# Half blocks of attention value products as 128x64 array tiles, with masks shared out between VectorE and GpSimd and a new instruction order

## The chip, the cores and the metric

The kernel runs on one core of one Trainium2 chip. The metric is the device time in microseconds (us) of one execution. The kernel before took 412.78 us, the median of three runs (412.25 to 413.30).

Names of engines, as in the profile: PE is TensorE (matmuls), PEld its weight loads, ACT is ScalarE, DVE is VectorE, POOL is GpSimd, SP is the queue from which most DMAs are issued. PSUM is the matmuls' output memory, here eight banks of 128 partitions x 512 float32.

## The reference

Four transformer layers on one sequence of 2048 rows of 512, in the order A, B, A, B, each with a residual and a layer norm ahead. Both use 32 heads of 16.

```python
def A(x, wqkv, wo):          # linear attention
    q, k, v = heads(x @ wqkv)
    phi = lambda t: where(t > 0, t + 1, exp(t)) + 1e-6
    kv = einsum("bhsd,bhse->bhde", phi(k), v)
    z = einsum("bhsd->bhd", phi(k))
    num = einsum("bhqd,bhde->bhqe", phi(q), kv)
    den = einsum("bhqd,bhd->bhq", phi(q), z)[..., None] + 1e-6
    return merge(num / den) @ wo

def B(x, wqkv, wo):          # causal sliding window of 256
    q, k, v = heads(x @ wqkv)
    scores = einsum("bhqd,bhkd->bhqk", q, k) * 16 ** -0.5
    keep = (i - j >= 0) & (i - j < 256)
    p = softmax(where(keep, scores, -1e9))
    return merge(einsum("bhqk,bhkd->bhqd", p, v)) @ wo

for layer, w, wo in ((A, A_wqkv, A_wo), (B, B_wqkv, B_wo)) * 2:
    x = x + layer(layernorm(x), w, wo)      # layernorm eps 1e-5
```

## The kernel before

**Tiling.** The rows are 16 blocks of 128 (`t`, `j`), all in SBUF as `xres`. Projections with the rows' features as weights are made by `tok` (L412, four matmuls of 512 columns a block) or, where the result is wanted transposed, by `feat` (L426, sixteen of 128 columns). A transposed normalised block comes from a DMA transpose on SP (L383), or for a few blocks from PE (L389).

**Norm** (`norm`). Statistics (L373) and their aggregate (L374) on DVE, the addition of the epsilon on POOL or DVE (L375), the power -0.5 on POOL (L376), subtraction and scaling on DVE (L377), then the transpose. In the attention layers the transposed block goes to `xT`, a ring of `ring_x` = 3.

**Attention layer B** (`middle`). For each block j: `front` makes the residual of the layer before, the norm, and the queries and keys of a later block; `b_v` the values; `b_scores` the scores. Scores are held with keys on partitions: a key block `b` of 64 keys stands twice (two heads a group) on the 128 partitions, and its exponentials `P` (ACT, L660) cover the 320 queries that can see it, of which the last 64 (the far edge) come from `b_far` (L690, L693, exponentials L703). Scores use array tiles of 32 rows, four beside each other; in the second B layer (`merged`) the first 32 and the last 64 query columns of a key block share a pass, in tiles of 32x64.

The causal edge of a key block is masked by `mk` (DVE, L668 and L713), the far edge by `mf` (POOL L721 or DVE L722).

`b_values` (L742) makes the outputs of query block j: for each of 16 pairs of heads, a sum over six key blocks in PSUM, with `P` as weights (128 keys-and-heads x 128 queries) and the values as 34 moving columns, two of which are the softmax sums. Of the six, the key block 2j+1 is seen only by the upper 64 queries and the key block 2j-4 only by the lower 64. Each key block's stretch in `P` has therefore 64 columns of zeros behind its 320 (row step 704, second block at 384), and both are read as full blocks of 128 with the zeros in the half that they don't reach. `consts` clears the zeros once (`c24`), and a step `zero` those of the fourth buffer of the second B layer (L816). Then DVE takes reciprocals (L753) and divides (L754), half of the heads at a time, and `b_out` transposes, multiplies by `wo` and adds the residual (L585).

**Order.** Nothing is decided at run time. Each step is a node of a graph (`Graph.add`) with the engines that may do it, its reads and writes, and a key. `place` reads a packed constant `TABLE`, which has for all steps the global order, the engine of each, and the PSUM bank of each tile; `synchronise` then puts in the waits on semaphores. Each engine's list is the order of the table. `place` adds one more dependence: a step on POOL that isn't in `SHORT` waits for the last step on DVE that is in `WIDE` and stands ahead of it in the order.

```python
        if o.eng == "POOL" and o.name not in SHORT and wide and wide not in o.deps:
            o.deps.append(wide)
        if o.eng == "DVE" and o.name in WIDE:
            wide = o
```

The first load order is `x0`, the key weight (512 KB), `x1`, `x2` and `x3`, the query weight, and so on. PE begins with matmuls on zeros (L998, L274) until data are there.

Of the kernel before, what the change touches and what calls it, by code (L numbers as in the profile page):

```python
# [8 lines left out]
ACT = mybir.ActivationFunctionType  # L9
ALU = mybir.AluOpType  # L10

P = 128
# [11 lines left out]
    same=0.0, gp=1, pe_first1=5, lat_t=4300, cap_s=8, cap_d=2, cap_e=6, mode=100, sem=35, ring_x=3, wait_s=200,  # L24
# [63 lines left out]
SHORT = ("eps", "pow", "c2", "c2b", "c11", "c12", "c13", "c14")  # L88
# [141 lines left out]
class Plan:  # L230


    def __init__(self, par):
        self.par = par
        self.g = Graph()
        self.n_phi = [0, 0]
        self.early = []
        self.closing = []
        self.build()
# [43 lines left out]
    def setup(self):  # L283
# [10 lines left out]
        seq += [xs(0, 1), w("wAk", "wA", "A_wqkv", 512, 1024), xs(1, 2), xs(2, 4), w("wAq", "wA", "A_wqkv", 0, 512), xs(4, 6), xs(6, 8), xs(8, 12)]  # L294
# [4 lines left out]
        for i, (n, f, b, r) in enumerate(seq):  # L299

            begun.append(self.load(n, f, b, r, key + i if i < 8 else 100.5 + 0.5 * i, begun[i - 4:i - 3] if i >= 7 else []))
# [10 lines left out]
        pool("c2b", zero(lambda: K.ones, 1.0), key + 2, 150, wr=[("ones",)])  # L312

    def consts(self, after):
# [23 lines left out]

        pool("c14", zero(lambda: K.tri, 1.0), 161, 200, wr=[("tri",)])
# [16 lines left out]
        for q in range(2):  # L356
            for k in range(4):
# [4 lines left out]
                self.g.add("wp", {"POOL": (810, 870), "ACT": act(512)}, move, 170 + q, rd=[("wBn",)], wr=[("wBp", q, k)], after=after)  # L362
        for s in range(3):
            clear("c24", lambda s=s: K.pb[:, s, :, :, 320:384], 1024, 180, 1000,
                  rd=[("wBp", q, k) for q in range(2) for k in range(4)] if s == 2 else [],
                  wr=[("pad", s)] + [("P", s, f) for f in range(4)])


    def norm(self, t, key, xn_slot, out, wr, by_pe):
# [3 lines left out]
        self.on("DVE", "stats", lambda e: e.bn_stats(K.stats[:, t, :], K.xres[:, t, :]), key, dve(512), rd=[("xres", t)], wr=[("stats", t)])  # L373
        self.on("DVE", "aggr", lambda e: e.bn_aggr(K.mv[:, t, :], K.stats[:, t, :]), key + 0.01, (66, 150), rd=[("stats", t)], wr=[("mv", t)])  # L374
        self.g.add("eps", {"POOL": (300, 330), "DVE": (66, 150)}, lambda e, eng: e.tensor_scalar(K.ve[:, t, :], K.mv[:, t, 1:2], LN_EPS, None, op0=ALU.add), key + 0.02, rd=[("mv", t)], wr=[("ve", t)])  # L375
        self.pow = self.on("POOL", "pow", lambda e: e.tensor_tensor(K.rs[:, t, :], K.ve[:, t, :], K.negh[:], ALU.pow), key + 0.03, (640, 690), rd=[("ve", t), ("negh",)], wr=[("rs", t)])  # L376
# [27 lines left out]
    def tok(self, name, t, lhs, rhs, rd, key):  # L404
# [3 lines left out]
        for h in range(2):  # L408
# [5 lines left out]
            self.pe(name, put, key - 0.001 * h, 2, 512, rd=rd, ps=[ps])  # L414
# [29 lines left out]
    def a_k(self, t, key):  # L444
        K = self
        xT = lambda c: K.XQ[:, c, t * P:(t + 1) * P]
        ps = self.tok("k", t, xT, lambda c: K.wA[:, c, 512:1024], [("XQ", t), ("wAk",)], key)
        self.phi(ps, lambda: K.pk[:, t, :], [("pk", t)], key + 0.1, 0)
# [12 lines left out]
    def a_kv(self, t, kv, z, key):  # L461
# [12 lines left out]
        self.pe("kv", put, key, 4, 128, occ=330, rd=[("pk", t), ("vA", t), ("ones",)], ps=[kv, z], after=self.closing)  # L474
# [112 lines left out]
    def b_qkv(self, t, s, key, key2):  # L587
# [4 lines left out]
        wk = [("wBp", 1, k) for k in range(4)]  # L592
        ps = self.feat("bq", t, lambda c, f: K.wBp[:, 0, c, f * P:(f + 1) * P], xT, rd + wq, key)
        self.copy("bqe", ps, lambda: K.XQ[:, :, t * P:(t + 1) * P], lambda ps=ps: K.ps(ps).rearrange("p (f n) -> p f n", f=4), key + 0.05, 512, wr=[("XQ", t)])
        key = key2
# [37 lines left out]

    def b_scores(self, j, b, fs, key):
# [21 lines left out]
        out = lambda h, w: bass_view(K.P(sl)[:, fs[0], h, 384 * b + skip:384 * b + skip + w], [[1408, 2 * n], [1, w]])  # L656
        for h in range(2):
# [4 lines left out]
            self.on("ACT", "ex", ex, key + 0.01 * h, act(2 * ns * n), wr=[("P", sl, f, b, h) for f in fs], rd=[("P", sl, f) for f in fs], ps=[ps[2 * h], ps[2 * h + 1]])  # L662
# [3 lines left out]
        def mk(e):  # L666
            x = bass_view(K.P(sl)[:, fs[0], 0, 384 * b:384 * b + 64], [[704, 4 * n], [1, 64]])
            return e.tensor_tensor(x, x, K.tri[:, 0, :].unsqueeze(1).to_broadcast([P, 4 * n, 64]), ALU.mult)  # L668

        self.on("DVE", "mk", mk, key + 0.02, dve(256 * n, "2x"), rd=[("P", sl, f, b, h) for f in fs for h in range(2)] + [("tri",)], wr=[("P", sl, f, b, 2) for f in fs])  # L670

    def b_far(self, j, key):
# [26 lines left out]
        for h in range(2):  # L699
            def ex(e, h=h):  # L700
                i = span(two(h), lambda x: [[128, 4], x, [64, 2], [1, 64]])
                o = bass_view(K.P(sl)[:, 0, h, 256:320], [[1408, 8], [384, 2], [1, 64]])
                return e.activation(o.rearrange("p (f g) b c -> p f g b c", g=2), i, ACT.Exp, bias=0.0, scale=0.25)  # L703

            self.on("ACT", "ex", ex, key + 0.01 * h, act(1024), wr=[("F", sl, h)], rd=[("P", sl, 0)], ps=[ps[2 * h], ps[2 * h + 1]])

        for fs in ((0, 1), (2, 3)) if merged else ():
            for b in range(2):
                def mk(e, b=b, fs=fs):
                    x = bass_view(K.P(sl)[:, fs[0], 0, 384 * b + 288:384 * b + 320], [[704, 8], [-256, 2], [1, 32]])  # L710
                    o = bass_view(K.P(sl)[:, fs[0], 0, 384 * b:384 * b + 64], [[704, 8], [32, 2], [1, 32]])
# [3 lines left out]
                self.on("DVE", "mk", mk, key + 0.02 + 0.01 * b + 0.2 * fs[0], dve(512, "2x"), rd=[("P", sl, f, b, h) for f in fs for h in range(2)] + [("F", sl, 0), ("F", sl, 1), ("tri",)],  # L715
                        wr=[("P", sl, f, b, 2) for f in fs] + [("near", sl, b, fs[0])])
        for b in range(2):
            def mk(e, eng, b=b):
                x = bass_view(K.P(sl)[:, 0, 0, 384 * b + 256:384 * b + 320], [[704, 16], [1, 64]])
# [7 lines left out]
    def b_values(self, j, h, key):  # L727
        K = self
        rp = self.rp
        ps = Tile(1, K.cls)  # L730
# [354 lines left out]
```

## Time and profile before

| what | value |
|---|---|
| median of three runs | 412.78 us (412.25 to 413.30) |
| span of the profiled execution, first to last instruction | 408.7 us |
| time of the profiled execution itself | not given apart from its span |
| clock granted to PE | 1.00 throughout |
| PE busy | 396.5 us in 7997 matmuls |
| ACT busy | 355.7 us |
| DVE busy | 343.9 us |
| POOL busy | 115.7 us |
| DMA | 37.88 MB moved, most of it in packets under 2 KB |

How to read it: "busy" is the time in which an engine had an instruction under way, and a matmul's duration holds some 0.17 us of latency that overlaps with the next ones. So the pace of matmuls is read from starts, not from durations. The chain of waits goes back from the last instruction to what released it; its shares say which engine's work set the end. Rows of groups give line, engine, operation, output and inputs, shape and count, then busy us and the mean ns of one, and behind the second bar the idle time before them.

### The profile page before, as it was taken

The page shows a single profiled execution, that of the slowest core. Times are in us where ns is not written, and L with a number is a line of the kernel's source. Part 1 is how long each engine was busy: PE and PEld are TensorE (multiplying, and loading weights), DVE is VectorE, ACT ScalarE, POOL GpSimd, SP SyncE. Part 2 cuts the span into 40 slices and gives each one's busy share as a digit, 9 for nine tenths or more (in the row PEclk, how much of TensorE's full clock was granted, in tenths as well). Part 3 has the DMA queues.
Part 4 walks back from the last instruction along what each step waited for, and adds up shares of the span by engine and source line. Part 5 has one row for each costly group of instructions (what it writes and reads, how often), then busy time and mean ns, then how long its engine had stood idle before and what let it go on. Part 6 is the DMA issues. An engine that isn't in the chain of part 4 may idle for free.

```text
span 408.7 us, 18140 instructions
## 1 busy us (share of the span) xinstructions
PE 396.5 (97%) x7997; PEld 262.5 (64%) x7997; DVE 343.9 (84%) x819; ACT 355.7 (87%) x466; POOL 115.7 (28%) x185
## 2 busy tenths in 40 slices
PE   8999999999999999999999999999999999999996
PEld 3654776766575576565566777676756766566664
DVE  7985899899999898997778879988898867876675
ACT  2998769999999999999998265999999899999992
POOL 5746422113342231521322102111213123432132
PEclk9999999999999999999999999999999999999999
DMA  7794025833342443344143100345224542352463
GB/s 246 189 197 80 2 62 146 126 92 83 67 108 43 126 101 82 93 101 101 42 68 60 25 2 28 80 107 109 55 76 103 133 69 60 104 120 79 102 135 105
DMA packets 67750, 37.88 MB, mean 93 GB/s; under 512 B 48248, under 2 KB 62840, under 8 KB 67672
## 3 DMA queue, kind: packets, MB, share of 16 engines
q1 hardware_dynamic: 67328, 35.80, 38.1%
q8 instruction: 63, 1.03, 1.1%
q0 software_dynamic: 336, 0.92, 0.6%
q14 instruction: 15, 0.12, 0.1%
q10 hardware_dynamic: 8, 0.00, 0.0%
HBM read 6.29 MB, written 2.10 MB: 21 GB/s over the span
## 4 chain that ended last, share of the span: by engine, by line
PE 66%; ACT 22%; DVE 7%; DMA 2%; issue 1%; POOL 0%; SPq 0%
PE ps L412 23%; PE ps L426 16%; ACT pb L660 14%; PE ps L742 11%; PE ps L650 6%; PE ps L492 3%; ACT pb L703 3%; ACT vp L660 2%; DMA xT<-xn 2%; PE ps L693 2%; ACT tE L435 1%; PE ps L690 1%; ACT vp L703 1%; PE ps L468 1%; DVE XQ L574 1%
## 5 line engine op out<-in xcount | busy, mean ns | idle before, releaser
L660 ACT ACTIVATE pb<-ps 128x1024 bf16<-128x1024 f32 (+3 forms) x224 | 197.8, 977 | 8.3 <-PE ps L650 7.3
L742 PEld LDWEIGHTS ps<-vB,pb 128*128 128x128 bf16 x2560 | 77.9, 96 | 11.3 <-issue 3.6
L742 PE MATMUL ps<-vB,pb 128*128 128x34 bf16 x2560 | 83.7, 177 | 0.8 <-issue 0.5
L426 PE MATMUL ps<-xT,wBp 128*128 128x128 bf16 x1024 | 70.2, 219 | 0.6 <-DMA xT<-xn 0.6
L426 PEld LDWEIGHTS ps<-xT,wBp 128*128 128x128 bf16 x1024 | 58.6, 98 | 12.3 <-issue 4.2
L721 POOL TENSOR_SCALAR_AFFINE_SELECT pb<-pb 128x1024 bf16<-128x1024 bf16 x35 | 40.7, 1162 | 67.9 <-DVE pb L713 28.8
L375 POOL TENSOR_SCALAR ve<-mv 128x1 f32<-128x1 f32 x38 | 9.7, 254 | 158.3 <-DVE mv L374 157.7
L435 ACT ACTIVATE tE<-ps 128x512 bf16<-128x512 f32 x64 | 38.1, 608 | 16.6 <-PE ps L412 9.1
L703 ACT ACTIVATE pb<-ps 128x1024 bf16<-128x1024 f32 x50 | 49.2, 1053 | 2.3 <-PE ps L693 1.3
L650 PE MATMUL ps<-XQ,kB 32*128 32x256 bf16 (+2 forms) x1024 | 48.0, 262 | 2.6 <-DVE vp L603 0.6
L412 PE MATMUL ps<-wA,XQ 128*128 128x512 bf16 x192 | 49.4, 379 | 0.2 <-DVE XQ L574 0.2
L585 DVE TENSOR_TENSOR xres<-ps,xres 128x512 bf16<-128x512 f32 x63 | 42.9, 683 | 7.9 <-PE ps L412 7.6
L376 POOL TENSOR_TENSOR rs<-ve,negh 128x1 f32<-128x1 f32 x64 | 38.6, 604 | 36.1 <-DVE ve L375 31.7
L373 DVE BATCH_NORM_STATS2 stats<-xres 128x6 f32<-128x512 bf16 x64 | 43.6, 683 | 2.4 <-DMA xres<-in_A_x_dram 1.7
L426 PE MATMUL ps<-XQ,wA 128*128 128x128 bf16 x512 | 35.1, 219 | 0.1
L412 PE MATMUL ps<-wBv,xT 128*128 128x512 bf16 x128 | 35.0, 381 | 0.0
L650 PEld LDWEIGHTS ps<-XQ,kB 32*128 32x128 bf16 x1024 | 15.3, 92 | 30.7 <-ACT pb L660 9.5
L426 PEld LDWEIGHTS ps<-XQ,wA 128*128 128x128 bf16 x512 | 30.4, 98 | 5.7 <-issue 0.6
L412 PE MATMUL ps<-M,XQ 128*128 128x512 bf16 x128 | 33.7, 380 | 0.1
L412 PE MATMUL ps<-wBo,oT 128*128 128x512 bf16 x124 | 33.2, 381 | 0.3 <-ACT pb L660 0.3
L668 DVE TENSOR_TENSOR pb<-pb,tri 128x512 bf16<-128x512 bf16 x68 | 28.1, 417 | 3.8 <-ACT pb L660 3.4
L412 PEld LDWEIGHTS ps<-wA,XQ 128*128 128x128 bf16 x192 | 16.6, 97 | 18.1 <-issue 1.0
(120 smaller groups left out, 566.8 us busy)
## 6 DMA issues: line engine op xcount, KB each, us to landing
vB<-vS SPq DMA_DIRECT2D x64, 136.0 KB, 2.6
kB<-vp SPq DMA_DIRECT2D x64, 128.0 KB, 2.2
wA<-in_A_wqkv_dram SPq DMA_DIRECT2D x3, 512.0 KB, 5.2
xres<-in_A_x_dram SPq DMA_DIRECT2D x2, 512.0 KB
pb<-in_B_wqkv_dram SPq DMA_DIRECT2D x1, 1024.0 KB, 5.5
out_dram<-xres SPq DMA_DIRECT2D x8, 128.0 KB, 3.2
out_dram<-xres POOLq DMA_DIRECT2D x7, 128.0 KB, 2.8
xres<-in_A_x_dram SPq DMA_DIRECT2D x3, 256.0 KB, 3.2
```

The lines of the kernel that those rows point to most:

```text
L373: self.on("DVE", "stats", lambda e: e.bn_stats(K.stats[:, t, :], K.xres[:, t, :]), key, dve(512), rd=[("xres", t)], wr=[("stats", t)])
L376: self.pow = self.on("POOL", "pow", lambda e: e.tensor_tensor(K.rs[:, t, :], K.ve[:, t, :], K.negh[:], ALU.pow), key + 0.03, (640, 690), r ...
L412: m = e.matmul(K.ps(ps), lhs(c), rhs(c), start=c == 0, stop=c == 3)
L426: m = e.matmul(K.ps(ps)[:, f * P:(f + 1) * P], w(c, f), xT(c), start=c == 0, stop=c == 3)
L435: self.on("ACT", "E", lambda e: e.activation(K.tE[:, s, :], K.ps(ps), ACT.Exp, bias=0.0), key, act(512), wr=[("tE", s)], ps=[ps])
L585: self.on("DVE", "res", lambda e: e.tensor_tensor(K.xres[:, t, :], K.ps(po), K.xres[:, t, :], ALU.add), key, dve(512), rd=[("xres", t)], w ...
L650: m = e.matmul(K.ps(two(gq // 2)[gq % 2])[:, ns * i:ns * i + ns], K.kB[rows, j % 4, 2 * f + b, :, :], K.XQ[rows, f, q:q + ns], start=True, ...
L660: return e.activation(out(h, ns).rearrange("p (f g) c -> p f g c", f=n), i, ACT.Exp, bias=0.0, scale=0.25)
L668: return e.tensor_tensor(x, x, K.tri[:, 0, :].unsqueeze(1).to_broadcast([P, 4 * n, 64]), ALU.mult)
L703: return e.activation(o.rearrange("p (f g) b c -> p f g b c", g=2), i, ACT.Exp, bias=0.0, scale=0.25)
L721: return e.affine_select(out=x, in_=x, compare_op=ALU.is_ge, fill=0.0, base=-2, pattern=[[0, 16], [-2, 64]], channel_multiplier=1)
L742: m = e.matmul(K.ps(ps)[:, 34 * u:34 * u + 34], K.P((b // 2) % rp)[:, f, gq % 2 * 2 + gq // 2, o:o + P], K.vB[:, (b // 2) % 4, b % 2, r, : ...
```

## The change

- **Half products.** `P` has no zeros any more (row step 640, second block at 320). `b_values` makes the four whole key blocks as before (`pv`), and then the two half ones as matmuls with 64 weight columns at `tile_position=(0, 0)` or `(0, 64)`, which write only 64 partitions of the output. They form a step of their own, `pw`, one for all 16 pairs of heads (two for the very last block). Both PSUM banks of a block are closed by it, and reciprocals and divisions of both come behind it. `c24` and the `zero` of the fourth buffer are gone. Where a buffer was lent out before, the first exponentials wait for the borrowers (`taken`).
- **Masks.** `mk` may be done by POOL too (`affine_select`; in the merged layer two of them).
- **Rings.** `xT` has five buffers in place of three; the layer's `front` runs five blocks ahead, with the keys split off (`b_k`, three ahead). `xn` has six buffers, `o` and `oT` three.
- **Epsilon.** The statistics get three more columns (0, 0, 512 x 1e-5), so that the aggregate gives variance + epsilon; the step L375 is gone. The statistics are a ring of eight.
- **Start.** The key weight is loaded in halves, behind `x0`, `x1` and `x2`; the key matmuls wait for each half by itself.
- **Order.** A new `TABLE` (2538 steps in place of 2568): order, engines, banks.

```diff
-    same=0.0, gp=1, pe_first1=5, lat_t=4300, cap_s=8, cap_d=2, cap_e=6, mode=100, sem=35, ring_x=3, wait_s=200,
+    same=0.0, gp=1, pe_first1=5, lat_t=4300, cap_s=8, cap_d=2, cap_e=6, mode=100, sem=35, ring_x=5, wait_s=200,
...
-SHORT = ("eps", "pow", "c2", "c2b", "c11", "c12", "c13", "c14")
+SHORT = ("pow", "c2", "c2b", "c2z", "c2e", "c11", "c12", "c13", "c14", "c16")
...
-        seq += [xs(0, 1), w("wAk", "wA", "A_wqkv", 512, 1024), xs(1, 2), xs(2, 4), w("wAq", "wA", "A_wqkv", 0, 512), xs(4, 6), xs(6, 8), xs(8, 12)]
+        def half(h):
...
+        seq += [xs(0, 1), xs(1, 2), xs(2, 3), half(0), half(1), xs(3, 4), w("wAq", "wA", "A_wqkv", 0, 512), xs(4, 6), xs(6, 8), xs(8, 12)]
...
+        pool("c2z", lambda e: e.memset(K.stats[:, :, 6:8], 0.0), key + 3, 100, wr=[("fold", 0)])
+        pool("c2e", lambda e: e.memset(K.stats[:, :, 8:9], D * LN_EPS), key + 4, 100, rd=[("fold", 0)], wr=[("fold",)])
...
-        for s in range(3):
-            clear("c24", lambda s=s: K.pb[:, s, :, :, 320:384], 1024, 180, 1000,
...
-        self.on("DVE", "aggr", lambda e: e.bn_aggr(K.mv[:, t, :], K.stats[:, t, :]), key + 0.01, (66, 150), rd=[("stats", t)], wr=[("mv", t)])
-        self.g.add("eps", {"POOL": (300, 330), "DVE": (66, 150)}, lambda e, eng: e.tensor_scalar(K.ve[:, t, :], K.mv[:, t, 1:2], LN_EPS, None, op0=ALU.add), key + 0.02, rd=[("mv", t)], wr=[("ve", t)])
...
+        self.on("DVE", "aggr", lambda e: e.bn_aggr(K.mv[:, t, :], K.stats[:, t % 8, :]), key + 0.01, (66, 150), rd=[("stats", t % 8), ("fold",)], wr=[("mv", t)])
...
+    def taken(self, j):
+
+        return self.borrowed if j == 2 and self.rp == 3 else self.summed if j == 3 and self.rp == 4 else []
...
-        def mk(e):
...
+        def mk(e, eng):
+            x = bass_view(K.P(sl)[:, fs[0], 0, 320 * b:320 * b + 64], [[640, 4 * n], [1, 64]])
+            if eng == "POOL":
+                return e.affine_select(out=x, in_=x, compare_op=ALU.is_ge, fill=0.0, base=1, pattern=[[0, 4 * n], [2, 64]], channel_multiplier=-1)
             return e.tensor_tensor(x, x, K.tri[:, 0, :].unsqueeze(1).to_broadcast([P, 4 * n, 64]), ALU.mult)
...
-        blocks = [(2 * j, 0), (2 * j + 1, -64), (2 * j - 1, 64), (2 * j - 2, 128), (2 * j - 3, 192), (2 * j - 4, 256)]
...
-                        o = 384 * (b % 2) + c
-                        m = e.matmul(K.ps(ps)[:, 34 * u:34 * u + 34], K.P((b // 2) % rp)[:, f, gq % 2 * 2 + gq // 2, o:o + P], K.vB[:, (b // 2) % 4, b % 2, r, :], start=i == 0, stop=i == len(blocks) - 1)
...
+        ps = [Tile(1, K.cls) for _ in range(2)]
+        whole = [(2 * j, 0), (2 * j - 1, 64), (2 * j - 2, 128), (2 * j - 3, 192)]
...
+        part = [(2 * j + 1, 0, 64)] + ([(2 * j - 4, 256, 0)] if j >= 2 else [])
...
+                        m = e.matmul(K.ps(ps[f // 2])[:, cols(f, gq)], stat(b, f, gq)[:, c:c + P], vals(b, f, gq), start=f % 2 == 0 and gq == 0 and i == 0, stop=False, skip_group_check=True)
...
+        for fs in ((0, 1), (2, 3)) if apart else (range(4),):
+            def put(e, fs=fs):
+                m = None
+                for f in fs:
+                    for gq in range(4):
+                        for b, c, r in part:
+                            m = e.matmul(K.ps(ps[f // 2])[r:r + 64, cols(f, gq)], stat(b, f, gq)[:, c:c + 64], vals(b, f, gq), start=False, stop=True, skip_group_check=True, tile_position=(0, r))
+                return m
...
-            self.b_qkv(t, t % ring, k - par["k_q"], k - par["k_kv"])
+            self.norm(t, k - par["k_ao"] + 0.3, t % 4, lambda: K.xT[:, t % ring, :, :], [("xT", t % ring)], t < par["pe_first"])
+            self.b_q(t, t % ring, k - par["k_q"])
...
         for j in range(T):
+            if j + ring < T:
+                front(j + ring)
             if j + 3 < T:
-                front(j + 3)
+                self.b_k(j + 3, (j + 3) % ring, base + j + 3 - par["k_kv"])
...
-            sb("xres", [T, D]); sb("XQ", [4, S]); sb("xn", [4, D]); sb("xT", [3, 4, P]); sb("pqd", [4, P])
+            sb("xres", [T, D]); sb("XQ", [4, S]); sb("xn", [6, D]); sb("xT", [5, 4, P]); sb("pqd", [4, P])
```

More of the change, by code (lines that the diff above doesn't have):

```diff
@@ L848, in middle @@
                 self.b_far(j, base + j + 0.8)
-            for h in range(2):
-                self.b_values(j, h, base + j + (h + 1) / 2 + par["k_pv"])
-            if not last:
-                self.closing = [self.g.ops[-1]]
+            self.b_values(j, base + j + 0.5 + par["k_pv"], last and j == T - 1)
             k = base + j + 1 + par["k_wo"]
```

244 lines of the change are left out of this document (126 added, 118 removed).

## The prediction

> **What bounds the kernel now.** I read the page first: busy shares, then the chain of waits.
>
> ```profile
> PE 396.5 (97%) x7997; PEld 262.5 (64%) x7997; DVE 343.9 (84%) x819; ACT 355.7 (87%) x466; POOL 115.7 (28%) x185
> ...
> PE 66%; ACT 22%; DVE 7%; DMA 2%; issue 1%; POOL 0%; SPq 0%
> PE ps L412 23%; PE ps L426 16%; ACT pb L660 14%; PE ps L742 11%; PE ps L650 6%; PE ps L492 3%; ACT pb L703 3%; ACT vp L660 2%; DMA xT<-xn 2%; PE ps L693 2%; ACT tE L435 1%; PE ps L690 1%; ACT vp L703 1%; PE ps L468 1%; DVE XQ L574 1%
> ```
>
> TensorE (PE) is nearly always busy and makes up two thirds of the chain that ends last; ScalarE (ACT), whose exponentials are L660 and L703, makes up a fifth. Next I cut the span where the exponentials of layer 2 begin and end (60.6 and 224.6 us) and those of layer 4 (257 and 401). The columns are window, length, then busy time of PE, PEld, DVE, ACT, POOL.
>
> ```profile
> 0.00:60.60 60.60, 59.17 (x593) 35.59 (x593) 49.76 (x140) 43.76 (x76) 31.07 (x64) 1.00 0.52 129
> 60.60:224.60 164.00, 161.76 (x3276) 104.34 (x3274) 146.37 (x349) 157.34 (x188) 44.74 (x65) 1.00 0.41 90
> 224.60:257.00 32.40, 32.40 (x506) 23.97 (x504) 27.78 (x62) 17.15 (x30) 3.47 (x8) 1.00 0.07 18
> 257.00:401.00 144.00, 138.96 (x3543) 95.82 (x3541) 116.13 (x262) 136.65 (x170) 35.36 (x46) 1.00 0.41 96
> ```
>
> Layers 2 and 4 take 308 of 408.7 us, and in both PE (99% and 97%) and ACT (96% and 95%) are full together. The first layer and the stretch between are PE alone. So work taken from PE counts in full only until ACT ends last; this decides how much of the change arrives.
>
> **The value products.** Of each block j >= 2, six key blocks of 16 matmuls make the output; two of the six have only 64 useful query columns and are now padded with zeros to 128. That is 14 x 32 + 2 x 16 = 480 half products a layer, 960 in all, of the 2560 + 320 matmuls on L742. Their number stays; they become tiles of 128x64 in the left and right half of the array. What does one cost before, and what does a tile cost?
>
> ```profile
> L742 PE MATMUL ps<-vB,pb x2560: 177/177/191, 74.5 to 402.9; 128*128 128x34 bf16 x197
> L742 PE MATMUL ps<-vB,vp x320: 177/177/191, 301.6 to 402.8; 128*128 128x34 bf16 x160
> ```
>
> ```profile
> 19.77 1.34 PE ps L426 x24
> ...
> 401.27 1.79 PE ps L742 x72
> ```
>
> ```profile
> 53.82 0.24 PE L554 MATMUL ps<-ones,eps 128*32 128x128 bf16 x4
> 53.89 0.40 PE L554 MATMUL ps<-XQ,zs 128*32 128x128 bf16 x16
> 54.22 0.61 PE L412 MATMUL ps<-M,XQ 128*128 128x512 bf16 x2
> ...
> 290.60 0.71 PE L693 MATMUL ps<-XQ,kB 32*64 32x64 bf16 x64
> 291.24 1.37 PE L742 MATMUL ps<-vB,pb 128*128 128x34 bf16 x48
> 292.54 0.37 PE L650 MATMUL ps<-XQ,kB 32*128 32x224 bf16 x8
> ```
>
> The 177 ns (least, median and most of one in ns stand behind the count) are latency; the pace is 1.79 us / 72 = 24.9 ns. The group of 48 takes 1.30 us to the start of the next, which has another tiling: 1.30 - 48 x 24.9 ns = 0.105 us is the price of a change of tiling.
>
> No 128x64 tile is in this trace, so it is bounded. The denominators (L554, 128x32 tiles) start at 53.82 and end with the next start at 54.22: 0.40 us less a change of 0.1 is 0.30 for 20, 15 ns each, where one matmul of 128 columns alone takes 1.34 / 24 = 56 ns. So column tiles with all 128 rows do run beside each other. If a left and a right tile together cost one full product, a half costs 24.9 / 2 = 12.5 ns. The merged scores (L693, 32x64 tiles, which also load 64 columns) take 0.64 - 0.1 = 0.54 us for 64: 8.4 ns each, the lower end. But each row group had 16 tiles to load in these 0.54 us, 34 ns a tile if left and right load in turn: the upper end. I take 14 ns, near the denominators, because only they use all rows. Saved: 960 x (24.9 - 14) = 10.5 us (15.8 at the lower end; at the upper 8.7 are lost).
>
> The new tiles form 33 groups of their own. Unpacking both order tables of the diff and reading them against the lists of steps, I count 334 changes of tiling on PE before and 377 after (21 of the new groups run straight into a score group): 43 x 0.105 = 4.5 us back. PE sheds 10.5 - 4.5 = 6.0 us. In the chain PE has 66% and ACT 22%, so I let three quarters of it arrive: **-4.5 us** (from -8.5 to +9.9). The half products also close both banks of a block, so that the first bank's division waits for all four groups, about 32 x 24.9 ns + 0.5 us later; behind it stand only the block's output transpose, for which there are three buffers in place of two, and PE's next user of that bank. I put 0 for it, since PE has other blocks' work between; without that it is 1.3 us in each of 32 blocks, of which the chain's 11% on L742 would carry some 4.5.
>
> The page "TensorEngine Tiling (Array Packing)" of the Trainium skill, section "Restrictions and Gotchas", says that column tiling excludes the fast weight load, and "TensorE: Matmul & The Clock Gate", section "LDWEIGHTS (loading the stationary operand)", puts a plain load at columns / 1.2 ns. An estimate from these pages, 53 ns a half product if the halves load in turn, makes the half products 960 x (53 - 24.9) = 27 us dearer, and the forecast about 431 us. The L693 rows (34 ns at the most) do not show so slow a load.
>
> **ACT, DVE, GpSimd.** The engine part of the new table gives, over the whole kernel: near masks (mk) 128 on DVE before, 56 on DVE and 72 on GpSimd after; far masks (mf) 16 on DVE and 40 on GpSimd before, 26 and 30 after; the epsilon step, 26 on DVE and 38 on GpSimd, is gone.
>
> ```profile
> L668 DVE TENSOR_TENSOR pb<-pb,tri x68: 360/416/756, 65.7 to 397.0; 128x512 bf16<-128x512 bf16 x68
> L713 DVE TENSOR_TENSOR pb<-pb,tri x44: 360/417/1944, 263.1 to 390.6; 128x512 bf16<-128x512 bf16 x44
> L722 DVE TENSOR_TENSOR pb<-pb,tri x15: 660/685/1026, 88.2 to 388.0; 128x1024 bf16<-128x1024 bf16 x15
> ```
>
> ```profile
> L375 POOL TENSOR_SCALAR ve<-mv x38: 209/223/568, 3.9 to 355.0; 128x1 f32<-128x1 f32 x38
> L375 DVE TENSOR_SCALAR ve<-mv x26: 131/146/155, 5.4 to 362.3; 128x1 f32<-128x1 f32 x26
> ```
>
> ```profile
> L721 POOL TENSOR_SCALAR_AFFINE_SELECT pb<-pb x35: 1137/1147/1341, 88.9 to 397.5; 128x1024 bf16<-128x1024 bf16 x35
> ```
>
> ```profile
> L401 ACT ACTIVATE XQ<-ps 128x512 bf16<-128x512 f32 x11 | 6.6, 604 | 1.1 <-PE ps L426 1.0
> ...
> L833 ACT ACTIVATE vp<-pb 128x1152 bf16<-128x1152 bf16 x3 | 3.5, 1159 | 0.0
> ```
>
> The first six rows have least, median and most of one in ns. DVE: -72 x 0.42 + 10 x 0.69 - 26 x 0.146 = -27, and about +2 for copies that come over from ACT and +2 for the longer aggregate of nine numbers: -23 us of 344, 7%. The chain has 7% on DVE, 28.6 us; 7% of that is **-2.0** (0 to -4).
>
> GpSimd: a near mask has half the elements of a far one (1147 ns), so 0.6 to 0.9 us, say 0.75: +72 x 0.75 - 10 x 1.15 - 38 x 0.22 = +34 us, to about 150 us, 37%. It is no bound, but it works in order: behind a mask stand the reciprocal roots (L376) of the norms and the other masks, and who waits are the value products of that block and the normalised rows of a later one. The mask itself comes 0.75 - 0.42 = 0.33 us later. With GpSimd at 0% of the chain I let five of the 72 come late, **+1.5**; the ends are 0 and 30 blocks x 0.33 = +10.
>
> ACT: five of its clears (1.1 us, as L833) and four short copies (0.6) go. The tables put nearly all of this outside layers 2 and 4; inside, ACT's list loses four copies and gains one exponential of phi in layer 2 (-2.1 us) and two short steps in layer 4 (-1.0). A quarter of 3.1 arrives: **-0.8**. In the first layer ACT is 72% busy, so its clears give **-0.3** (0 to -1.2).
>
> **The ring of transposes and the start.**
>
> ```profile
> 171.33 2.56 DMA xT<-xn
> ...
> 325.09 4.03 DMA xT<-xn
> ```
>
> ```profile
> 6.33 0.39 POOL ve L375
> ...
> 6.80 0.64 POOL rs L376
> ...
> 8.56 0.40 PE ps L389 x4
> ```
>
> Twice the chain waits for a transposed block, 6.6 us together. With five slots in place of three, residual, norm and transpose of a block are issued two blocks earlier, past nothing new on SP but other transposes and key and value moves. These waits go; what is late next is PE or ACT work that stands close behind, since both were mostly busy meanwhile, so I take half: **-3.3** (0 to -6.6). The new waits on `taken` (the first exponentials in a buffer lent out before) find their releasers done a block or more earlier: 0. At the start, the epsilon step stands on the way to the first matmul: 6.80 - 6.33 = 0.47 us, **-0.5**. The key weight, now in halves behind three x blocks, is covered by the same norms, after which the last transposes before the first key product run at 8.56 us; without that cover, the two x blocks more ahead of it cost about what the shorter norm brings, and the term is 0.
>
> **Sum.** -4.5 - 0.8 - 0.3 - 2.0 + 1.5 - 3.3 - 0.5 = -9.9 us, from a span of 408.7 to 398.8. The only time beside the span is the median of 412.78, 4.1 us above it; kept, that gives 402.9, said as 403.
>
> **Rivals.** *ACT ends last.* For it: a stretch in which only exponentials are on the chain.
>
> ```profile
> 202.85 8.85 ACT pb L660 x10
> ```
>
> Here ten follow each other at 0.885 us, and the number of exponentials (312) does not change. Then PE's 6 us become idle time, and only ACT's 3.1, the clears' 0.3 and the start's 0.5 arrive: 408.9. Against it: ACT has 6.7 and 7.4 us idle in layers 2 and 4, which relief on DVE and earlier transposes can fill.
>
> *The halves load in turn (slower).* At 34 ns a half product, PE's term is (8.7 + 4.5) x 0.75 = +9.9 instead of -4.5: 403 + 14.4 = 417. It decides from the point where PE's term eats the other -5.4: 960 x (c - 24.9 ns) + 4.5 = 7.2 us, c = 27.7 ns. For it, L693 alone; against it, the denominators.
>
> *Masks late on GpSimd.* With the upper end, +10 for +1.5, the time is 411.5. For it: GpSimd already holds 1.15 us steps which come behind DVE's masks (L721). Against it: 0% of the chain.
>
> **How the numbers follow.** The forecast has 0.62, ACT 0.18, late masks 0.10, halves in turn 0.10. About 0.3%, 1.2 us, is what a measurement of this kernel can tell from no change: faster is below 411.5. The forecast's own range is 397 to 408. Downward, the cheaper half product (-4.0) and the rest of the ring (-3.3) reach 395.5; upward, ACT and late masks reach 411.5. Outside lie the halves in turn and parts of the rest. Faster: 0.62 + 0.17 + 0.02 = 0.81; same 0.07; slower 0.12.
>
> **What would show it.** Right: the new line's groups of 32 take 0.4 to 0.5 us to the next start less a change; 2880 value matmuls in two shapes; DVE at about 321 us, GpSimd about 150, ACT about 348; no stretch over 2 us on DMA xT<-xn in the chain; first transpose near 8.1 us. Wrong: a pace over 27.7 ns in the half products; ACT over 97% in both layers with PE idle before scores; value products waiting for GpSimd.

## The result, and the profile after

The changed kernel takes 413.79 us (median of 20 runs), the kernel before 412.24 us (20 runs on the same chip): a ratio of 1.0054, 95% interval 1.0033 to 1.0076. It is 2.2 us slower by the ratio, where 9.9 us less were forecast. (The ratio compares means and leaves one slow execution of the kernel before out, so it is not that of the two medians.) The granted clock isn't the reason: the executions at 0.999 or more alone have medians of 413.56 us (14 of the changed kernel) and 411.65 us (37 of the kernel before, from the later batches).

Page of the changed kernel, busy shares and the chain by engine and by line. Its profiled execution took 417.4 us (span 415.6), above the median, with a clock of 0.96 between 80 and 120 us; where stages are compared below, a run at full clock stands in.

```profile
PE 387.2 (93%) x7925; PEld 259.4 (62%) x7997; DVE 325.1 (78%) x735; ACT 351.1 (84%) x457; POOL 148.3 (36%) x242
...
PE 58%; ACT 26%; DVE 7%; DMA 4%; issue 3%; POOL 1%; SPq 0%; POOLq 0%
PE ps L413 19%; ACT pb L670 16%; PE ps L427 16%; PE ps L760 7%; PE ps L660 5%; ACT pb L715 4%; PE ps L772 3%; ACT vp L670 2%; PE ps L494 2%; ACT tE L436 2%; PE ps L705 1%; DMA kB<-vp 1%; DMA XQ<-vp 1%; PE ps L702 1%; DMA oT<-o 1%
```

The engines got lighter, if by less than was counted: DVE 343.9 to 325.1, ACT 355.7 to 351.1; GpSimd took on 32.6. (72 of PE's 7997 records are missing here, so its own sum is too low.) PE's share of the chain fell, and ACT, DMA and issue took it over. DVE and ACT are lighter, and the end is no earlier.

**The new tiles.** Timeline of the changed kernel: a group of 32 half products (L772), and one of 16 in an early block, where only one of the two halves exists.

```profile
72.87 0.36 PE L760 MATMUL ps<-vB,pb 128*128 128x34 bf16 x8
73.15 0.68 PE L772 MATMUL ps<-vB,pb 128*64 128x34 bf16 x16
...
403.98 0.68 PE L772 MATMUL ps<-vB,pb 128*64 128x34 bf16 x32
404.60 0.24 PE L660 MATMUL ps<-XQ,kB 32*128 32x64 bf16 x8
```

Groups of the same kernel by shape, with the mean ns of one before the last bar:

```profile
L760 PEld LDWEIGHTS ps<-vB,pb 128*128 128x128 bf16 x1712 | 53.9, 96 | 10.5 <-issue 4.2 <-ACT pb L670 1.0 <-DVE vp L609 0.5
...
L772 PEld LDWEIGHTS ps<-vB,pb 128*64 128x64 bf16 x848 | 18.7, 112 | 1.8 <-issue 0.6 <-POOL pb L726 0.4
...
L772 PE MATMUL ps<-vB,pb 128*64 128x34 bf16 x848 | 22.0, 184 | 0.3 <-POOL pb L726 0.3
```

Both groups last 0.68 us, one matmul's latency of 0.18 included. Where left and right alternate, 31 intervals take 0.50 us: 16.1 ns a half product, or 32 ns for a left and a right one together. Where one half is alone, 15 intervals take the same 0.50 us: 33 ns, as long as a pair, and more than the 24.9 of a full product. A weight load of these tiles is longer too on average, 112 ns against 96 (latency included), with half the columns. The Trainium skill ("TensorE: Matmul & The Clock Gate", section "LDWEIGHTS (loading the stationary operand)") puts a plain load at columns / 1.2 ns; by it, an estimate, halves that load in turn would take 53 ns each, and neither pace here is as slow. That column tiling goes without the fast weight load, as the Trainium skill says ("TensorEngine Tiling (Array Packing)", section "Restrictions and Gotchas"), fits the lone halves' 33 ns, but no run here separates the load from the rest.

**Who waits.** Before, then after: DVE's wait for the sums of an output block (total us, times, longest).

```profile
DVE rc L753 <- PE ps L742: 10.9, 17, 1.4
```

```profile
DVE rc L782 <- PE ps L772: 22.5, 23, 1.9
```

**Transfers in the chain of the changed kernel**, those over 1.8 us behind the first load:

```profile
31.99 5.44 DMA XQ<-vp
...
166.14 3.72 DMA kB<-vp
...
203.41 1.90 DMA kB<-vp
...
406.07 3.96 DMA oT<-o
```

The two waits for `xT` are gone, and four others stand there. (The account above of the first loads needs a correction. In the trace of the kernel before, four loads of x, blocks 0 to 5, are issued ahead of the key weight, whose load is issued at 2.79 us; in the changed kernel the same six blocks come in five loads, and the first half of the key weight follows at 3.25 us. So the key weight was not moved behind x blocks by the change.)

### The profile page after: what moved, and what is told of

Read it like the earlier page. It is cut to its first block, busy times and chain, and to the rows that moved or that the text cites. A ratio compares the mean times of both kernels' runs of the same rounds, so it can differ in the third digit from the quotient of the medians.

```text
span 415.6 us, 18085 instructions
## 1 busy us (share of the span) xinstructions
PE 387.2 (93%) x7925; PEld 259.4 (62%) x7997; DVE 325.1 (78%) x735; ACT 351.1 (84%) x457; POOL 148.3 (36%) x242
## 4 chain that ended last, share of the span: by engine, by line
PE 58%; ACT 26%; DVE 7%; DMA 4%; issue 3%; POOL 1%; SPq 0%; POOLq 0%
PE ps L413 19%; ACT pb L670 16%; PE ps L427 16%; PE ps L760 7%; PE ps L660 5%; ACT pb L715 4%; PE ps L772 3%; ACT vp L670 2%; PE ps L494 2%; ACT tE L436 2%; PE ps L705 1%; DMA kB<-vp 1%; DMA XQ<-vp 1%; PE ps L702 1%; DMA oT<-o 1%
## 5 line engine op out<-in xcount | busy, mean ns | idle before, releaser
L377 POOL TENSOR_TENSOR rs<-mv,negh 128x1 f32<-128x1 f32 x64 | 38.2, 596 | 81.2 <-DVE mv L376 78.5
L760 PEld LDWEIGHTS ps<-vB,pb 128*128 128x128 bf16 x1712 | 53.9, 96 | 10.5 <-issue 4.2
L760 PE MATMUL ps<-vB,pb 128*128 128x34 bf16 x1712 | 59.0, 177 | 0.5 <-ACT pb L670 0.3
L679 POOL TENSOR_SCALAR_AFFINE_SELECT pb<-pb 128x512 bf16<-128x512 bf16 x41 | 27.5, 670 | 69.1 <-ACT pb L670 39.4
L413 PE MATMUL ps<-wA,XQ 128*128 128x512 bf16 x175 | 46.3, 380 | 3.4 <-DMA XQ<-vp 0.8
L375 DVE BATCH_NORM_STATS2 stats<-xres 128x6 f32<-128x512 bf16 x64 | 43.6, 683 | 3.2 <-DMA xres<-in_A_x_dram 2.5
L737 POOL TENSOR_SCALAR_AFFINE_SELECT pb<-pb 128x1024 bf16<-128x1024 bf16 x27 | 31.0, 1147 | 29.5 <-ACT pb L715 11.3
L413 PE MATMUL ps<-wBv,xT 128*128 128x512 bf16 x109 | 29.7, 380 | 5.0 <-issue 1.1
L413 PE MATMUL ps<-wBo,oT 128*128 128x512 bf16 x106 | 28.6, 379 | 4.4 <-DMA oT<-o 1.1
L726 POOL TENSOR_SCALAR_AFFINE_SELECT pb<-pb 128x256 bf16<-128x256 bf16 x46 | 20.2, 463 | 33.5 <-DVE pb L729 10.0
L782 DVE RECIPROCAL rc<-ps 128x16 f32<-128x16 f32 x64 | 14.3, 239 | 22.7 <-PE ps L772 22.5
```

Of the source, the lines that this page charges most:

```text
L375: self.on("DVE", "stats", lambda e: e.bn_stats(K.stats[:, t % 8, 0:6], K.xres[:, t, :]), key, dve(512), rd=[("xres", t)], wr=[("stats", t ...
L413: m = e.matmul(K.ps(ps), lhs(c), rhs(c), start=c == 0, stop=c == 3)
L679: return e.affine_select(out=x, in_=x, compare_op=ALU.is_ge, fill=0.0, base=1, pattern=[[0, 4 * n], [2, 64]], channel_multiplier=-1)
L737: return e.affine_select(out=x, in_=x, compare_op=ALU.is_ge, fill=0.0, base=-2, pattern=[[0, 16], [-2, 64]], channel_multiplier=1)
L760: m = e.matmul(K.ps(ps[f // 2])[:, cols(f, gq)], stat(b, f, gq)[:, c:c + P], vals(b, f, gq), start=f % 2 == 0 and gq == 0 and i == 0, stop ...
```

## The experiments

All differences below come from ratios to the kernel before in the same batch. Against the changed kernel they are the difference of two ratios, times 412.24 us; the half-widths of the two intervals are added in squares.

**PE lighter, in either kernel.**

```diff
  x1, changed kernel
-                        for b, c, r in part:
+                        for b, c, r in part if gq == 3 and f % 2 else ():
  x2, kernel before
+                        if gq < 2 and c in (-64, 256):
+                            continue
...                      (the condition for stop is adapted to it)
```

> The changed kernel, of whose half products only 4 of each group of 32 are done (2 of 16 in the groups of one bank); the others are left out, and all steps, waits and changes of tiling stay. PE sheds 28 x 16 ns = 0.45 us in each of 30 groups, 13 us. Theory A (the new order waits, PE less the bound): 4 to 8 us of it arrive, 406 to 410 us. Theory C (ACT ends last): under 3 us arrive, 411 to 413 us. If PE were the bound throughout: 401 us.

> The kernel before, of whose half products half are done (two of the four head pairs of each group leave their two half blocks out); nothing else changes. PE sheds 16 x 25 ns = 0.4 us in each of 28 blocks, 12 us in all with the first blocks. It is the counterpart of the run that took 13 us of half products from the changed kernel and gained 1.8 us. If PE's work sets the time of the kernel before: 401 to 405 us. If the fixed order and its waits on ACT keep the time whatever PE sheds (theory C): 409 to 412 us.

x1: 412.0 us, ratio 0.9962 (0.9935 to 0.9989): 3.8 ± 1.4 us below the changed kernel, for 13.9 us less of PE's busy time. x2: 412.95 us, ratio 1.0015 (0.9989 to 1.0041): nothing arrives (0.6 ± 1.1 us more) of 480 x 24.9 ns = 12 us. x1 lies at the edge between its two expectations, x2 in the second of its two. Shares of the chain in x1, then x2:

```profile
PE 49%; ACT 42%; DVE 4%; issue 2%; DMA 1%; POOL 0%; SPq 0%; POOLq 0%
```

```profile
PE 43%; ACT 41%; DVE 10%; DMA 3%; issue 3%; POOL 0%
```

In both, ACT's share goes from 26 (x1) or 22% (x2) to over 40%: by the chain, what PE sheds becomes mostly waiting for exponentials. In x1 DVE's wait for the sums also falls from 22.5 to 12.4 us, so its 3.8 us can come from earlier sums as well as from less work. PE's 66% of the chain did not say that two thirds of a saving arrive.

**ACT lighter; both; all three.**

```diff
  x3: exponentials of scores 1/16 narrower (the rest left out)
+        nw = ns - ns // 16 if self.merged or j >= 3 else ns
-                i = span(two(h), lambda x: [[ns, n], x, [1, ns]])
+                i = span(two(h), lambda x: [[ns, n], x, [1, nw]])
...              (the output is narrowed in the same way)
  x13: x1 and x3     x23: x2 and x3, kernel before     x134: x13, and
-  e.bn_stats(K.stats[:, t % 8, 0:6], K.xres[:, t, :])
+  e.bn_stats(K.stats[:, t % 8, 0:6], K.xres[:, t, 0:256])
```

> The changed kernel with score exponentials one sixteenth narrower (from the fourth block of layer 2 on, and in all of layer 4); the last columns of each are left out. ACT sheds 104 x 53 + 128 x 47 ns = 11.5 us. Theory C (ACT ends last): 6 to 11 us arrive, 402 to 408 us. Theory A (waits between engines in the new order, no one engine the bound): 1 to 4 us, 410 to 413 us.

> The changed kernel with both reliefs that brought little by themselves: few half products (PE sheds 13 us, 1.8 us arrived) and score exponentials one sixteenth narrower (ACT sheds 11.5 us, 1.4 us arrived); the half products and last columns are left out. Theory C2 (PE and ACT are both the bound and take turns: what one sheds, the other keeps): 7 to 12 us arrive, 402 to 407 us. Theory A (the fixed order waits on something else, DVE, DMA or bank hand-over): the two small gains add at most, 3 us, 410 to 411 us.

> As the run with both reliefs, and the layer norm's statistics are taken over half of each row, which takes about 64 x 0.3 = 20 us from DVE. Theory C2 (PE and ACT alone): 0 to 2 us below that run. Theory A with DVE as the third engine that takes turns: 4 to 10 us below it.

> The kernel before with half of its half products left out (PE sheds 12 us, nothing arrived) and score exponentials one sixteenth narrower (ACT sheds 11.5 us). Theory C2: 7 to 12 us faster than before, 400 to 405 us. Theory A: 0 to 3 us, 409 to 412 us.

x3: 412.35 us, 2.0 ± 1.5 below the changed kernel for 8.9 us less of ACT (11.5 expected). x13: 406.43 us, 7.8 ± 1.6 below; the two alone sum to 5.8, so that they bring more together is suggested, not shown. x134: 406.37 us; DVE, 13.8 us lighter on the page than in x13, adds nothing measurable (0.2 ± 1.7). x23: 410.06 us, 2.8 ± 1.2 below the kernel before, far from the 7 to 12 that two engines taking turns were to bring; DVE's share of its chain is 20%, where the kernel before has 7%. Chain of x3, then x13:

```profile
PE 74%; ACT 11%; DVE 6%; DMA 4%; issue 3%; SPq 1%; POOL 1%; POOLq 0%
```

```profile
PE 52%; ACT 25%; DVE 8%; DMA 6%; issue 4%; POOL 3%; SPq 1%; POOLq 0%
```

With ACT lighter the chain moves to PE (74%). In the changed kernel each of the two engines takes over a larger part of the chain when the other is relieved. Even of both reliefs together (22.8 us) a third arrives there, and in the kernel before about an eighth.

**The half tiles taken back.** y2 leaves the order and makes every half product a full one:

```diff
-  e.matmul(K.ps(ps[f // 2])[r:r + 64, cols(f, gq)], stat(b, f, gq)[:, c:c + 64], vals(b, f, gq), ..., tile_position=(0, r))
+  e.matmul(K.ps(ps[f // 2])[:, cols(f, gq)], stat(2 * j + 1, f, gq)[:, 0:P], vals(b, f, gq), ...)
```

> The changed kernel, in which each half product is a full 128x128 product on other weights of the same buffer (the wrong columns: it is a price, not a value), as before the change, but in the place in the order where the half ones stand. No tile of 128x64 and none of its changes of tiling are left. By the rows, 896 paired half products go from 16.1 to about 25 ns (+8 us) and up to 43 changes of tiling at 0.1 us go (-4.4 us): PE +3.6 us. Theory (PE's saving was taken up by ACT): 0 to +1.5 us against the changed kernel, 413.5 to 415.5. Rival one (PE's saving arrives by three quarters, as predicted): +2.7 us or more. Rival two (the change of tiling in front of a half group is what costs the time): -1 us or more, below 412.8.

417.25 us, ratio 1.0104 (1.006 to 1.0148): 2.1 ± 2.0 us above the changed kernel. So in this order the tiles alone are worth about 2 us, and all that is left of the change costs 4.3 us (2.5 to 6.1) against the kernel before. This splits the result in two. Two reservations: the order was made for the shorter steps, so some of the 4.3 us may be its misfit to longer ones; and at a clock of 0.999 or more alone the medians are 417.15 us (5 executions of y2) and 413.56 (14 of the changed kernel, another batch), 3.6 us apart, so the tiles may be worth nearer to 4. Rival two of that run (the change of tiling is what costs the time) is ruled out; rival one (2.7 us or more) is not.

**Shorter masks on GpSimd**, order unchanged:

```diff
-  pattern=[[0, 4 * n], [2, 64]]      on 64 columns
+  pattern=[[0, 4 * n], [2, 16]]      on 16 columns (merged layer: 8 of 32)
```

> The changed kernel, in which GpSimd's near masks treat only the first quarter of their columns (the rest of each mask is left out). Order, engines, waits and number of steps are unchanged. GpSimd's 72 near masks (0.67 us, or twice 0.46 us, in the changed kernel's rows) should fall to some 0.35 us and twice 0.3 us: about 20 us less on GpSimd, and every such mask 0.3 us earlier. Theory (PE and ACT are loaded alike and each takes over what the other sheds; GpSimd's masks are not what costs the time): 0 to -1.5 us against the changed kernel, 412.5 to 414. Rival (masks late on GpSimd eat the gain of the half products): -3 us or more, below 411.

414.14 us, ratio 1.0036 (1.0003 to 1.0069): 0.7 ± 1.6 below the changed kernel, though GpSimd is 23 us lighter. So the length of GpSimd's masks explains at most some 2.4 us, and by the centre less than 1; what their place on GpSimd costs otherwise isn't tested by it. Page and stages of y1 and y2 have all matmul records and a clock of 1.00, so they can be set beside the kernel before. Windows end at the first and last exponential of layers 2 and 4; columns as in the prediction.

Before:

```profile
0.00:61.10 61.10, 59.67 (x604) 35.85 (x605) 50.26 (x141) 43.78 (x77) 31.07 (x64) 1.00 0.52 129
61.10:224.20 163.10, 160.86 (x3264) 103.92 (x3263) 145.47 (x347) 157.32 (x188) 44.74 (x65) 1.00 0.41 90
224.20:257.70 33.50, 33.40 (x517) 24.35 (x516) 28.88 (x64) 17.67 (x32) 3.47 (x8) 1.00 0.07 18
257.70:401.00 143.30, 138.36 (x3532) 95.59 (x3531) 115.43 (x261) 136.12 (x170) 35.36 (x46) 1.00 0.41 97
401.00:408.70 7.70, 4.20 (x88) 2.74 (x85) 3.84 (x9) 0.78 (x3) 1.08 (x2) 1.00 0.34 103
```

y1, the changed kernel with shorter masks:

```profile
0.00:62.10 62.10, 60.36 (x603) 35.70 (x604) 51.01 (x134) 42.12 (x74) 28.62 (x59) 1.00 0.49 135
62.10:226.10 164.00, 160.61 (x3263) 103.27 (x3264) 136.53 (x305) 156.58 (x186) 46.94 (x81) 1.00 0.40 87
226.10:259.30 33.20, 33.01 (x541) 24.45 (x539) 28.70 (x64) 16.81 (x30) 4.86 (x8) 1.00 0.12 26
259.30:401.90 142.60, 136.20 (x3519) 92.33 (x3516) 103.08 (x225) 135.03 (x168) 43.16 (x91) 1.00 0.42 96
401.90:410.80 8.90, 4.33 (x80) 2.57 (x78) 4.07 (x10) 0.38 (x1) 1.43 (x3) 1.00 0.26 76
```

y2, layers 2 and 4, and the sum (PE, PEld, DVE, ACT, POOL):

```profile
62.20:228.60 166.40, 162.42 (x3263) 105.70 (x3262) 137.44 (x305) 156.89 (x186) 59.28 (x81) 1.00 0.41 85
...
261.90:406.70 144.80, 137.96 (x3518) 94.36 (x3516) 103.46 (x225) 135.14 (x168) 53.03 (x91) 1.00 0.41 95
...
sum 415.30, PE 398.62 PEld 263.48 DVE 325.04 ACT 351.36 POOL 147.93; mean PE 79.72 PEld 52.70 DVE 65.01 ACT 70.27 POOL 29.59
```

In y1, layers 2 and 4 together are as long as before (306.6 against 306.4), though DVE is 21 us lighter in them and ACT 1.8. PE's busy time there fell by 2.4 us and its idle time rose by 2.6, from 7.2 to 9.8. The 2.1 us of span that y1 has more than before lie at the edges: 1.0 in the first layer and 1.2 behind the last exponential, less 0.3 between. y2's span is 6.6 us longer than before: 2.1 of PE's busy time (398.6 against 396.5) and 4.5 of its idle time (16.7 against 12.2). The profiled executions aren't equally quick, though. Nearly everywhere the time is 1.7 to 1.8 us longer than the span; by that, an estimate, the one of the kernel before took some 410.4 us, nearly 2 below its median, and that of y1 is as far below its own, but that of y2 is at its median. So some 2 of the 6.6 us are a matter of which execution was profiled.

**Masks put back on DVE in the new order (u1), and moved to GpSimd in the old order (p2).**

```diff
  u1: TABLE, engine part: the 72 near masks of GpSimd -> DVE, far masks as before the change
  p2, kernel before: TABLE, engine part: the same 72 near masks DVE -> GpSimd
+            if eng == 'POOL':
+                return e.affine_select(out=x, in_=x, compare_op=ALU.is_ge, fill=0.0, base=1, pattern=[[0, 4 * n], [2, 64]], channel_multiplier=-1)
```

> The changed kernel in its own order, with all 128 near masks on DVE and the far masks on the engines of before. Theory A: 412 to 416 us, as the changed kernel, or a little slower, since its order was made for other engines. Theory B: 405 to 410 us. Theory C: 412 to 415 us.

> The kernel before with one part of the change alone: the 72 near masks that the changed kernel has on GpSimd go there; order, far masks and all else as before. Theory B (GpSimd masks are late, since they take 0.67 us for DVE's 0.42): 3 to 10 us slower than before. Theory A and C: within 2 us, the 30 us that DVE sheds paying for the later masks.

u1: 432.91 us, 17.3 ± 2.2 above the changed kernel. p2: 418.29 us, ratio 1.0147 (1.0114 to 1.018), 6.1 us above the kernel before. Page and chain of u1, then chain of p2:

```profile
PE 388.3 (90%) x7925; PEld 258.8 (60%) x7997; DVE 344.0 (80%) x797; ACT 353.0 (82%) x457; POOL 105.4 (25%) x151
...
PE 52%; ACT 23%; DVE 17%; DMA 3%; issue 3%; POOL 1%; SPq 1%
```

```profile
PE 53%; ACT 21%; DVE 13%; POOL 7%; issue 3%; DMA 2%; SPq 0%; POOLq 0%; DVEq 0%
```

In u1, 19 us more of DVE's busy time cost 17, with DVE at 80%: longer steps in this fixed list were paid nearly in full, while x134 got nothing for shorter ones. Moving the masks costs time in both directions, as it would if either order is fitted to its own engines, so neither run prices the masks as such.

**The old order for the changed steps (o1; o1m with the masks on GpSimd), and both kernels in a third order (r1, r2).**

```diff
  o1, o1m: TABLE: each step at its place and on its engine before the change; pw behind the block's last pv;
           steps for which no PSUM bank was free put off
  r1, r2:  TABLE: single steps moved up or down the list wherever the measured durations made its end earlier;
           engines and banks kept
```

> The changed program with the instruction order, engines and masks of the kernel before: its steps in the old sequence, each group of half products right behind the block's last whole products, the key weight loaded where it was, masks as before (128 near masks on DVE). Theory A (the edits are sound, and the new order gives their gain back as waits): faster than the kernel before, 404 to 409 us. Theory B (the GpSimd masks are at fault): also faster, since no near mask is on GpSimd. Theory C (PE's saving does not arrive whatever the order, ACT ends last): 410 to 413 us.

> The same as the run with the old order, but with the engines of the masks of the changed kernel (72 near masks on GpSimd). Theory A: within 1 us of the run with all near masks on DVE. Theory B (GpSimd masks are late): 3 to 8 us slower than that run. Theory C: 410 to 413 us as there.

> The changed kernel with its steps, engines and PSUM banks as they are, in another global order: many small moves of single steps, each kept where the durations in this case's rows made the whole list end earlier. Theory (the parts of the change bring about nothing by themselves, and what is left is how well one in-order list fits them): 408 to 412, and no lower than the kernel before treated in the same way (next run) by more than 1 us. Rival (the change is worth several us and only its order hides that): 3 us or more below the kernel before treated in the same way.

> The kernel before with its steps, engines and PSUM banks as they are, in another global order, found in the same manner and with as many moves tried as for the changed kernel (run before this). Theory: 406 to 411, that is about as far below the kernel before as the reordered changed kernel is below the changed one. Rival (the change is worth several us and only its order hides that): 3 us or more above the reordered changed kernel.

o1 501.18 us and o1m 502.43 us; r1 429.4 us, ratio 1.0379 (1.0331 to 1.0427), and r2 428.44 us, ratio 1.0401 (1.0347 to 1.0455). Waits of o1 (ACT's, DVE's):

```profile
ACT pb L670 <- PE ps L660: 68.0, 58, 3.5
```

```profile
DVE rc L782 <- PE ps L772: 62.4, 31, 4.6
```

I read these waits so: in o1 the sums stay open until `pw`, which holds back scores and so exponentials, and half products that close both banks need an order of their own. That isn't shown: with steps put off for want of a bank, and a granted clock of 0.93 on average, the 88 us can't be shared out, and o1 against o1m (1.3 us) is within its error. r1 and r2 miss their expected gain by far: both end some 16 us later than the kernel before, with more DMA in the chain (r1, then r2):

```profile
PE 58%; ACT 23%; DMA 10%; DVE 5%; issue 2%; SPq 1%; ACTq 0%
```

```profile
PE 59%; ACT 15%; DMA 12%; DVE 12%; issue 1%; SPq 1%; DVEq 0%
```

So measured durations of steps didn't lead to a better order; that the waits for transfers are what they lacked is suggested by these shares, not shown. What can be read: treated alike, the two kernels differ by 0.9 ± 3.0 us, so the rival (3 us or more hidden by the order alone) finds no support, though 3 us are just within the error, and the order alone moves either kernel by more than the whole change does.

**Two steps moved (s1), and the epsilon folded in the old order (p3).**

```diff
  s1: TABLE: the load wBv behind the last transpose of the first layer;
             the output product of block 14 (bout) behind the first of block 15
  p3, kernel before:
-  self.g.add("eps", ...)
+  stats [13, 9] with the columns 0, 0, 512 * 1e-5; pow reads the aggregate
```

> The changed kernel with two steps moved in its order: the load of the layer-B value weight goes behind the last transpose of the first layer (which in the trace landed 5.4 us after its issue, beside that load), and the output product of block 14 behind the first one of block 15 (it waited 1.1 us for its transpose at the end). If these two places hold the lost time as the trace says: 1.0 to 2.2 us faster than the changed kernel, 411.5 to 413 us. If what follows is late anyway: no change, 413 to 414.5 us.

> The kernel before with one part of the change alone: the epsilon folded into the aggregate, the 64 epsilon steps gone, all else in the old order (statistics in a ring of 13). Each norm is 0.25 to 0.47 us shorter, 38 x 0.22 us leave GpSimd and 26 x 0.146 DVE. The prediction's step for the start: 0.5 us faster at least. If the norms stand on the way elsewhere too: 1 to 4 us faster, 408 to 411 us. Theory A (the old order fits the old durations): no change within 1 us.

s1: 413.42 us, 0.6 ± 1.3 below the changed kernel. Its chain holds no `XQ<-vp` and no `oT<-o` any more, 9.4 us in the chain of the changed kernel:

```profile
1.73 2.26 DMA xres<-in_A_x_dram
...
161.92 3.94 DMA kB<-vp
```

So a wait for a long transfer in the chain did not bring its length when it was removed. p3: 413.18 us, ratio 1.0028 (1.0005 to 1.0051): in the old order the shorter norm brings nothing, rather a loss of 1.2 us.

## Why the prediction was wrong

**Most of what was counted came out.** The new groups take 0.62 us to the next start, a change included; there are 2880 value matmuls in two shapes; DVE has 325 us (321 said, so it shed 19 of the 23), GpSimd 148 (150), ACT 351 (348, so it shed some 5 of 8); no wait for `xT` over 2 us; the last transposes before the first key product run at 7.95 us (8.1 said). The paired halves are not as slow as the rival in which they load in turn: 16.1 ns, below the 27.7 at which it decides. That a left and a right tile together cost one full product did not come out either: a pair takes 32 ns against 24.9. The work was nearly right; its worth in time was not.

**The step that failed most: a saving priced by an engine's or a wait's share of the chain,** with no term for the new order beside it. The prediction saw that PE and ACT are full together in layers 2 and 4, and still let three quarters of PE's saving arrive, 7% of DVE's share of the chain and half of the ring's waits. That is behind nearly every term of the sum.

- The terms outside PE and the masks (ACT and clears -1.1, DVE -2.0, ring -3.3, start -0.5) were -6.9, with the masks' +1.5 -5.4. In y2 they stand together with what the sum put at 0 (both banks closed at once, the waits on `taken`) or gave no term (the new order), and all of it measures +4.3 (2.5 to 6.1): 9.7 us of the 12.1 us between forecast and result. How much of that is savings that did not arrive, and how much the terms of 0, no run separates. Part by part, as far as the runs show it: relief of DVE brought nothing measurable where it was tried (x134); the ring's waits went and others stood there (chain after), whose removal brings 0.6 ± 1.3 (s1); the epsilon step brought no gain in the old order (p3), and the first exponential of layer 2 comes 1.0 us later in y1 in spite of the earlier start. "What is late next" was asked for the ring, and half was guessed. At the start, the two x blocks more ahead of the key weight were a misreading: the same six blocks stand ahead of it in both kernels.
- PE's term was -4.5; by y2 it is -2.1 ± 2.0 (3.6 less by the executions at full clock), the smaller part of the miss. First, it was mis-sized: 16.1 ns where 14 was taken, 33 ns for the 64 halves that stand alone, so 896 x 8.8 - 64 x 8.1 ns = 7.4 us instead of 10.5, less 4.5 for the changes of tiling: 2.9 instead of 6.0. Second, where more was taken from PE not three quarters arrived but 3.8 of 13.9 us (x1), or none of 12 (x2). y2 alone doesn't show that second point: PE is 4.1 us busier in it than in y1, and about half of that, or more, is in the time.

**The rivals.** *ACT ends last* (408.9) is nearest in kind: ACT's share of the chain grew, and x1 and x2 show relief of PE turning into waits for ACT. But ACT alone isn't the bound either (x3), and besides the masks no rival had the rest of the change costing time. *Masks late on GpSimd*: y1 leaves their length at most some 2.4 us; p2's 6.1 us hold for the old order alone. That GpSimd's busy time came out is in part luck: the 0.75 us a mask is 0.65 to 0.67 us for a single one and twice 0.46 for the merged ones, which average to 0.75. The prediction's cover for closing both banks ("PE has other blocks' work") held only in part: DVE's wait for sums doubled, from 10.9 to 22.5 us. The prediction said that without this cover some 4.5 us more would be due, which is about the size of what y2 leaves; but what the wait is worth in time was not separated.

**What stays open.** The 4.3 us aren't traced to one wait. y2's page shows PE's idle time (+4.5 us) and some busier PE (+2.1), spread over both attention layers and the edges, with some 2 us too many for the quick execution of the kernel before. The new order, the joint closing of the banks and the deeper ring come together in it, and an order can't be undone alone (o1). No version ran faster than the kernel before with all of its work done.

## What to carry to other kernels

In these fixed lists, with two engines both about 95% busy or more in the attention layers, work taken from one of them arrived for a quarter (x1, x3) or not at all (x2), while work added cost from half of its length (y2, PE) to nearly all of it (u1, DVE at 80%). Before crediting a saving, ask what the other engine does in that time, and put 0 as the base and the share of the chain at most as the upper end. A removed wait is worth at most the distance to the next one. Where a change comes with a rewritten order, give the order a term of its own, with both signs, and at least as wide as all the other terms.

## What the hardware showed beyond that

- Tiles of 128x64 with 34 moving columns take 16.1 ns each when left and right alternate and about 33 ns when one side stands alone, so a lone half takes as long as a pair; a full 128x128 product takes 24.9. A lone half is dearer than a padded full one.
- On GpSimd a mask costs by its elements above a fixed part: 463 ns for 256 columns, 670 for 512 (changed kernel):

```profile
L679 POOL TENSOR_SCALAR_AFFINE_SELECT pb<-pb 128x512 bf16<-128x512 bf16 x41 | 27.5, 670 | 69.1 <-ACT pb L670 39.4 <-DVE xn L378 6.8 <-DVE tE L437 5.7
...
L726 POOL TENSOR_SCALAR_AFFINE_SELECT pb<-pb 128x256 bf16<-128x256 bf16 x46 | 20.2, 463 | 33.5 <-DVE pb L729 10.0 <-DVE pb L738 7.1 <-DVE rc L782 4.8
```

In y1, whose masks are shorter, one takes 341 ns for 128 columns. Two masks of 256 cost 0.26 us more than one of 512, which the estimate of 0.75 us a mask had left out.
